# Re-timing three transfers of a recurrent attention step: query transposes, normed rows, value copies

## The chip, the cores and the metric

The kernel runs on one core of one Trainium2 chip. The metric is the device time of one execution in microseconds (us), as the median of several runs. Beside it stands one profiled execution, whose trace has every instruction of the engines (PE multiplies matrices, DVE and ACT do elementwise work, POOL and SP issue most of the transfers) and every packet of the 16 DMA engines.

## The reference

The input is one sequence of 2048 tokens of width 640. The first half of the layer is attention with a recurrent memory. The tokens are cut into 64 segments of 32. Each segment is joined with 8 memory rows, and attention with 32 heads of width 128 runs over these 40 rows. The output rows of the 8 memory places are the memory of the next segment, so the segments run one after another. The second half is a feed-forward block with a gate.

```python
for s in range(n_seg):
    h = jnp.concatenate([mem, xs], axis=1)      # 8 memory rows, 32 tokens
    q, k, v = (jnp.einsum('btd,dhe->bhte', h, W) for W in (Wq, Wk, Wv))
    scores = jnp.einsum('bhqe,bhke->bhqk', q, k) * scale
    o = jnp.einsum('bhqk,bhke->bhqe', _softmax(masked scores), v)
    o = jnp.einsum('bhte,hed->btd', o, Wo)
    mem = o[:, :M, :]
...
h = x + attention(layernorm(x)); h2 = h + W_down(relu(gate) * up)
```

(The weights' loop is drawn together here; the mask lets a row see the memory and the tokens up to itself.)

## The kernel before

The work is one program, written out for each engine as a list of operations. `_Graph.solve` (line 61) gives each operation the semaphore waits that it needs from the keys that it reads and writes: a write of a buffer waits until every earlier reader is done, and where the reader is a DMA, until the DMA has landed. Each engine runs its own operations in the order of the program text. There is no planner: the order in the text sets the order on each engine and in each DMA queue.

**The steps.** The loop at line 905 runs once per segment (a step). A step projects a tile of 32 columns, which holds the 8 memory rows and 24 "rider" tokens of later segments, because the memory is the only thing that the step has to wait for. So the keys, queries and values of ordinary tokens are made ahead of their segment and kept in rings of three segments: `Kr` (keys), `Qr` (queries), `Vr` (values). A block of 128 tokens is spread over four steps: 4 times 24 riders are 96, and the other 32 (the "extra" tokens, `act_e`) are projected in `extra_units` (line 858): their keys in the third step (s%4==2), their queries in the fourth, their values in the first step of the next block. In what follows, first to fourth step means s%4 = 0 to 3.

**One step in order.** PE projects the keys into two PSUM banks; ACT and DVE copy them to `tok[0]` and `tok[1]` (`to_tok`, line 429). SP transposes these 256 KB by DMA into `KS` (line 936), then the attention rows of the step before into `oT` (`trans_ox`, line 709). PE projects the queries, which go to `tok[2]` and `tok[3]`, and then the values, which go to `Vp`. `scores` (line 562) needs `KS`, and the ring slots of keys and queries of this segment. `exp_mem` (line 581) takes the exponentials of the memory's scores and masks them on DVE into `Pbd`: these are the memory probabilities. `exp_x` does the tokens' scores. Then `pv_mem`, the transposes of its result, `wo_pass` (line 638, 128 small matmuls) which gives the next memory, and `pv_x` (line 680) for the tokens.

**The rider queries.** `trans_q` (line 458) transposes `tok[2:4]` by DMA on SP's queue into `QS`, and `evac_q` (line 485) copies the riders from `QS` to `Qr` on ACT. In the first and second step (`qlate`) the transpose is issued at the end of the step and its evacuation is put on the list `late_k`, run in the next step behind the query copy. In the third and fourth step it is issued right behind `trans_ox` (line 949) and evacuated at the end of the value part (line 971).

**The rider values.** `v_riders` (line 492) issues DMAs from `Vp` to `Vr`: four, or eight where the 24 riders straddle two segments, as they do in the second and third step. All are issued by POOL.

**The extra keys.** In the third step, `evac` (line 874) copies the extra tokens' keys to `tok[2]` and `tok[3]`, and SP transposes them straight into `Kr`.

**The normed rows.** In the third step a block of input rows is normed on DVE (`row_scale`, line 382) into `xt`, and SP transposes it into `at` (line 1020), behind `pv_x` in the text; POOL copies it to the activations in the next step (`ln1_back`, line 518). For four blocks, in steps 32, 36, 40 and 44, the first step has a row block of the feed-forward part at the same place (`EARLY`, line 889).

**Instructions of PE.** `align` (line 138) pads PE's list with weight loads that do nothing, so that every 256th instruction falls at a chosen place of a step's `wo_pass` (`MARKS`, line 228).

Of the kernel before, what the change touches and what calls it, by code (L numbers as in the profile page):

```python
# [208 lines left out]
def build_kernel(nc, A_x, A_mem0, A_Wq, A_Wk, A_Wv, A_Wo, A_seg_len, B_W_gate, B_W_up, B_W_down, out):  # L209
    _, S, D = A_x.shape  # L210
    M = A_mem0.shape[1]
# [4 lines left out]
    NSEG = S // SEG  # L216
# [145 lines left out]
    def dma_t(dst, src, r, w):  # L362
        add("sp", lambda e: e.dma_start_transpose(dst, src), r=r, w=w, dma=True)
# [18 lines left out]
    def row_scale(src, skey, n, dst, dkey):  # L382
        add("dve", lambda v: v.tensor_scalar(dst[0:n, :], src[0:n, :], mv[0:n, 0:1], rs[0:n, 0:1], ALU.subtract,
                                             ALU.mult), r=[skey, ("mv",), ("rs",)], w=[dkey])
# [44 lines left out]
    def to_tok(b, t, eng):  # L429
        copy_op(eng, tok[t][:, :], bank(b), [B(b)], [("tok", t)])  # L430
# [58 lines left out]
    def seg_slot(s):  # L489
        return (s - 2) % (RING // SEG)  # L490

    def v_riders(t0, n, after=()):

        done = 0
        while done < n:
            t = t0 + done
            q, o = seg_slot(t // SEG), t % SEG
            m = min(n - done, SEG - o)
            for g in range(4):
                a, z = 32 * g + M + done, 32 * (g ^ 1) + o  # L500
                dma(Vr[q][z:z + m, :, :], Vp[a:a + m, :, :], r=[("Vp", 0), ("Vp", 1), ("Vp", 3), ("Vp1",), ("Vr1", q)] + list(after),
                    w=[("Vr", q, g, o)], eng="pool")
            done += m

    def vr_keys(q):
# [75 lines left out]
    def exp_mem():  # L581
        add("act", lambda a: a.activation(ap(om, 0, [[8, 2], [16, 8], [1, 8]]), s_view(0, M), ACTF.Exp,
                                          scale=SCALE), r=[B(P0), B(P1)], w=[("om",)])
        for i in range(2):
            add("dve", lambda v, i=i: v.tensor_tensor(ap(Pbd, 256 * i, [[32, 8], [16, 2], [1, 16]]),
                                                      ap(om, 0, [[16, 8], [0, 2], [1, 16]]),
                                                      ap(mbd, 32 * i, [[0, 8], [16, 2], [1, 16]]), ALU.min),
                r=[("om",), ("mbd",)], w=[("Pbd", i)])

    def exp_x():  # L590
        add("act", lambda a: a.activation(ap(Px, 0, [[32, 2], [64, 8], [1, 32]]), s_view(M, M + SEG),  # L591
# [83 lines left out]
    def store_attn(src, skey, s):  # L675

        dma(bass.AP(attn_d, SEG * s * D, [[160, 4], [D, SEG], [1, 160]]), src[:].rearrange("p c j -> p (c j)"), r=[skey],
            w=[("attn", s)], eng="pool")
# [179 lines left out]
    def extra_units(s):  # L858

        b, r = (s - 2) // 4, (s - 2) % 4
        t0 = 64 + 128 * b + 96
        if b < 0 or r == 3 or t0 >= S:
            return None, None, None
        a, ks = act_e[b % 2], [("acte", b % 2)]
        q = seg_slot(t0 // SEG)
        j = (1, 0, 2)[r]

        def part(n):
            project(a, ks, j, (0, 1), BQ, PARTS[n], j // 2)

        def evac():
            for i, e in enumerate(("act", "act")):
                if j == 2:
                    to_v(BQ[i], Vr[q], i, ("Vr", q), e)
                else:
                    to_tok(BQ[i], 2 + i, e)
            if j == 1:  # L880
                dma_t(Kr[q][:].rearrange("p h t -> p (h t)").rearrange("p (k r) -> p k r", r=128), tokp[1][:, :],
                      [("tok", 2), ("tok", 3)], [("Kr", q)])

        def fin():
            trans_q()
            late_q.append(lambda: evac_q(QS, ("QS",), t0, 32, 0, "act"))
        return part, evac, (fin if j == 0 else None)
# [17 lines left out]
    for s in range(NSEG):  # L905
# [20 lines left out]
        if s > 0:  # L926
            a, ks, kn = pass_act(s)
            t0, nr = rider_tokens(s)
            project(a, ks, 1, (0, 1), BQ, (0, 1), spare=16)
            ks = ks + kn  # L930
            project(a, ks, 1, (0, 1), BQ, (2, 3, 4), spare=24)
            to_tok(BQ[0], 0, "act")
            to_tok(BQ[1], 1, "dve")
            if last:
                break
            dma_t(KS[:].rearrange("p h t -> p (h t)").rearrange("p (k r) -> p k r", r=128), tokp[0][:, :],
                  [("tok", 0), ("tok", 1)], [("KS",)])
            trans_ox()
            for f in late:
                f()  # L940
            late = []
            project(a, ks, 0, (0, 1), (P0, P1), spare=40)
            to_tok(P0, 2, "act")
            to_tok(P1, 3, "dve")
            for f in late_k + late_q:
                f()
            late_k, late_q = [], []
            qlate = nr and s % 4 < 2
            if nr and not qlate and s < NSEG - 2:
                trans_q()  # L950
            loads()
            project(a, ks, 2, (0, 1), (P2, P3), (0, 1), spare=16)
            if s == NSEG - 2:
                trans8(tok[2], ("tok", 2), tok[3], ("tok", 3), T0)
                copy_op("dve", Qr[:, :, q, 0:M], slots(T0, 0, M), [B(T0)], [("Qm", q)])
                evac_q(slots(T0, 0, SEG), B(T0), t0, nr, M, "act")
            else:
                pick_mem(T0)
                copy_op("dve", Qr[:, :, q, 0:M], bank(T0)[:, 0:256].rearrange("p (h t) -> p h t", t=M), [B(T0)], [("Qm", q)])
            if nr:  # L960
                evac_k(KS, ("KS",), t0, nr, M, "dve")
            project(a, ks, 2, (0, 1), (P2, P3), (2, 3, 4), spare=24)
            to_v(P3, Vp, 1, ("Vp", 3), "dve")
            to_v(P2, Vp, 0, ("Vp", 0), "act", 0, 2)
            scores(s)
            exp_mem()
            to_v(P2, Vp, 0, ("Vp", 1), "act", 2, 4)
            exp_x()
            if nr:
                v_riders(t0, nr)  # L970
                if s < NSEG - 2 and not qlate:
                    evac_q(QS, ("QS",), t0, nr, M, "act")
        units, evac, nfin = extra_units(s)
        woe = s % 4 == 1 and s >= 5
# [1 line left out]
        def filler(n):  # L976
            if units:
                units(n)
            if woe:
                woe_pass(BQ[0], WPARTS[n])  # L980
# [12 lines left out]
        n = n_rows(nb) if s % 4 == 2 and ln else 128 if e2b is not None else 0  # L993
        if n:
            row_scale(xt, ("xt",), n, xt, ("xt",))
        filler(4)
        if evac:
            evac()
# [13 lines left out]
        if s >= 1:  # L1012
            wo_rows(T1, wtok[s % 2], ("wtok", s % 2), "act")
            store_attn(wtok[s % 2], ("wtok", s % 2), s - 1)
            if qlate and s < NSEG - 2:
                trans_q([("act", (s + 1) // 4 % 2, (s + 1) % 4, "m")])
                late_k.append(lambda t0=t0, nr=nr: evac_q(QS, ("QS",), t0, nr, M, "act"))
        pv_x(s, P0)
        if n:
            dma_t(chunks_of(at[:, :])[:, :, 0:n], xt[0:n, :], [("xt",)], [("at",)])  # L1020
            if s % 4 == 2:
                late.append(lambda nb=nb: ln1_back(nb, chunks_of(at[:, :]), [("at",)], "pool"))
        if nfin:
# [229 lines left out]
```

## Time and profile before

| | us |
|---|---|
| median of 3 runs | 1100.82 |
| lowest and highest run | 1099.63 and 1101.9 |
| profiled execution | 1100.57 |
| its span, first to last instruction | 1098.8 |
| PE busy | 1057.8 (96% of the span) |
| DVE, ACT, POOL busy | 608.4, 362.6, 291.5 |
| DMA moved | 121.60 MB |

The recurrence fills the span from about 50 to 911 us (the last `pv_x`, line 690, starts at 910.9); the feed-forward part follows. Lines are of kernel.py, and a helper's line stands for all of its uses: L464 and L466 are the copies on ACT and DVE, L360 is a plain DMA, L363 a transposing one, L400 and L422 are matmuls of the projections. "SPq" is SP's issue of a DMA: its length is that of the issue, not of the transfer. The table of DMA issues gives the median time from issue to landing.

### The profile page before, as it was taken

The page shows a single profiled execution, that of the slowest core. Times are in us where ns is not written, and L with a number is a line of the kernel's source. Part 1 is how long each engine was busy: PE and PEld are TensorE (multiplying, and loading weights), DVE is VectorE, ACT ScalarE, POOL GpSimd, SP SyncE. Part 2 cuts the span into 40 slices and gives each one's busy share as a digit, 9 for nine tenths or more (in the row PEclk, how much of TensorE's full clock was granted, in tenths as well). Part 3 has the DMA queues.
Part 4 walks back from the last instruction along what each step waited for, and adds up shares of the span by engine and source line. Part 5 has one row for each costly group of instructions (what it writes and reads, how often), then busy time and mean ns, then how long its engine had stood idle before and what let it go on. Part 6 is the DMA issues. An engine that isn't in the chain of part 4 may idle for free.

```text
span 1098.8 us, 55766 instructions
## 1 busy us (share of the span) xinstructions
PE 1057.8 (96%) x27875; PEld 511.8 (47%) x23292; DVE 608.4 (55%) x1673; ACT 362.6 (33%) x792; POOL 291.5 (27%) x585
## 2 busy tenths in 40 slices
PE   4789999999999999999999999999999999999999
PEld 2454545444545444545444544444445455444444
DVE  3245656565656565666656665565656554553522
ACT  1213333333433433333333333333333332231211
POOL 1023233333333232323232323242323243000000
PEclk9989999999999999999999999999999999999999
DMA  9946464546464545556556556554455548132100
GB/s 360 387 91 113 87 108 88 104 90 104 91 101 90 103 90 100 94 109 111 112 104 112 108 112 107 101 97 93 94 101 93 92 96 313 43 80 72 31 18 24
DMA packets 285882, 121.60 MB, mean 111 GB/s; under 512 B 261392, under 2 KB 275300, under 8 KB 285648
## 3 DMA queue, kind: packets, MB, share of 16 engines
q1 hardware_dynamic: 265920, 93.92, 40.9%
q0 software_dynamic: 19312, 23.86, 9.6%
q8 instruction: 201, 3.29, 1.3%
q14 instruction: 33, 0.27, 0.1%
q10 hardware_dynamic: 416, 0.26, 0.1%
HBM read 36.79 MB, written 7.19 MB: 40 GB/s over the span
## 4 chain that ended last, share of the span: by engine, by line
PE 90%; DMA 5%; SPq 3%; DVE 1%; issue 1%; ACT 0%; DVEq 0%
PE ps L422 25%; PE ps L400 23%; PE ps L644 13%; PE ps L1051 11%; PE ps L666 3%; PE ps L690 3%; PE ps L572 3%; SPq L360 3%; PE ps L1092 3%; DMA Wo<-in_A_Wo_dram 3%; PE ps L609 2%; PE ps L453 2%; DMA QS<-tok 1%; DMA KS<-tok 1%; PE ps L624 1%
## 5 line engine op out<-in xcount | busy, mean ns | idle before, releaser
L422 PE MATMUL ps<-W,act_r 128*32 128x512 bf16 x4292 | 404.8, 385 | 6.5 <-DMA W<-in_A_Wv_dram 2.6
L400 PE MATMUL ps<-W,act_r 128*32 128x512 bf16 x3588 | 359.0, 379 | 0.0
L360 POOL DMA_DIRECT2D Vr<-Vp x376 | 187.2, 505 | 345.5 <-ACT Px L591 280.6
L422 PEld LDWEIGHTS ps<-W,act_r 128*32 128x32 bf16 x4292 | 126.0, 97 | 257.7 <-issue 157.2
L464 ACT ACTIVATE tok<-ps 128x512 bf16<-128x512 f32 x192 | 110.8, 593 | 228.4 <-PE ps L400 200.4
L644 PE MATMUL ps<-Wo,oT 128*32 128x160 bf16 x8064 | 156.9, 235 | 6.2 <-DMA Wo<-in_A_Wo_dram 3.1
L466 DVE CAST tok<-ps 128x512 bf16<-128x512 f32 x131 | 90.5, 691 | 130.1 <-PE ps L400 109.5
L644 PEld LDWEIGHTS ps<-Wo,oT 128*32 128x32 bf16 x8064 | 143.8, 98 | 26.6 <-DVE oT L466 16.8
L422 PE MATMUL ps<-W,act_e 128*32 128x512 bf16 x900 | 89.8, 381 | 0.0
L400 PE MATMUL ps<-W,act_e 128*32 128x512 bf16 x900 | 89.4, 379 | 0.0
L555 DVE STREAM_TRANSPOSE TBf<-ps 128x64 f32<-128x64 f32 (+1 forms) x128 | 33.6, 263 | 93.2 <-PE ps L644 93.2
L705 DVE TENSOR_TENSOR ox<-ps,rx 128x512 bf16<-128x512 f32 x128 | 82.5, 686 | 2.2
L464 ACT ACTIVATE Qr<-QS 128x512 bf16<-128x512 bf16 (+3 forms) x107 | 69.7, 680 | 38.4 <-DMA QS<-tok 38.4
L360 POOL DMA_DIRECT2D attn_d<-wtok x62 | 46.4, 748 | 130.8 <-ACT wtok L464 130.8
L464 ACT ACTIVATE Vp<-ps 128x256 bf16<-128x256 f32 (+1 forms) x126 | 48.5, 385 | 81.5 <-PE ps L400 79.0
L1066 DVE TENSOR_TENSOR hT<-g,ps 128x512 bf16<-128x512 bf16 (+1 forms) x56 | 38.5, 688 | 47.3 <-PE ps L1051 43.4
L1051 PE MATMUL ps<-xn2T,Wg 128*128 128x512 bf16 x260 | 64.6, 379 | 0.0
L1051 PE MATMUL ps<-xn2T,Wu 128*128 128x512 bf16 x260 | 64.6, 379 | 0.0
L1064 ACT ACTIVATE g<-ps 128x512 bf16<-128x512 f32 (+1 forms) x56 | 32.4, 592 | 91.6 <-PE ps L1051 91.6
L466 DVE CAST Vp<-ps 128x512 bf16<-128x512 f32 x64 | 44.2, 691 | 28.3 <-PE ps L400 22.3
L1092 PE MATMUL ps<-Wd,hT 128*128 128x320 bf16 x210 | 57.2, 299 | 0.0
L400 PE MATMUL ps<-Wd,hT 128*128 128x320 bf16 x210 | 57.2, 299 | 0.0
(121 smaller groups left out, 1151.8 us busy)
## 6 DMA issues: line engine op xcount, KB each, us to landing
Vr<-Vp POOLq DMA_DIRECT2D x124, 48.8 KB, 1.9
W<-in_A_Wk_dram SPq DMA_DIRECT2D x2, 2560.0 KB, 13.4
W<-in_A_Wq_dram SPq DMA_DIRECT2D x2, 2560.0 KB, 29.0
W<-in_A_Wv_dram SPq DMA_DIRECT2D x2, 2560.0 KB, 27.7
Wo<-in_A_Wo_dram SPq DMA_DIRECT2D x2, 2560.0 KB, 28.5
xt<-in_A_x_dram SPq DMA_DIRECT2D x30, 160.0 KB, 2.7
Vr<-Vp POOLq DMA_DIRECT2D x128, 32.5 KB, 2.3
at<-attn_d SPq DMA_DIRECT2D x16, 160.0 KB, 3.4
```

The costliest lines, as they stand in the source:

```text
L360: add(eng, lambda e: e.dma_start(dst, src), r=r, w=w, dma=True)
L400: return pe.add_instruction(mybir.InstMatmult(name=nc.get_next_instruction_name(), engine=mybir.EngineType.PE, ins=[pe.lower_ap(rhs), pe.l ...
L422: ins = pe.matmul(*a, start=(c == 0), stop=(c == DC - 1), skip_group_check=True)
L464: add("act", lambda a: a.activation(dst, src, ACTF.Copy), r=r, w=w)
L466: add("dve", lambda v: v.tensor_copy(dst, src), r=r, w=w)
L555: add("dve", lambda v, lo=lo, hi=hi: v.transpose(TBf[:, lo:hi, :].rearrange("p c t -> p (c t)"), src[:, 32 * lo:32 * hi]), r=[wkey], w=[(" ...
L572: i = pe.matmul(bank((P0, P1)[g % 2])[p:p + (M if a else 32), 40 * k:40 * k + 40], lh, Qr[:, h, q, :], start=True, stop=True, skip_group_c ...
L644: i = pe.matmul(bank(bk)[32 * gg:32 * gg + 32, 0:160], src[:, hb, :], w[:, gg], start=(hb == ORDER[0]), stop=(hb == ORDER[31]), skip_group ...
L705: add("dve", lambda v, kh=kh: v.tensor_tensor(ox[:, :, kh, :], src[:, :, kh, 0:128], ap(rx, kh, [[2, 4], [0, 128]]), ALU.mult), r=[B(b0 + ...
L1051: ins = pe.matmul(bank(bk), w[:, c, lo:lo + 128], xn2T[par][:, :, c, :], start=(c == 0), stop=(c == DC - 1))
L1066: add("dve", lambda v: v.tensor_tensor(hT[par][lo:128, j, :], g1[gi][lo:128, :], bank(bu)[lo:128, :], ALU.mult), r=[B(bu), ("g1", gi)], w= ...
L1092: i = pe.matmul(*a, start=(j == 0), stop=(j == FC - 1), skip_group_check=True)
```

## The change

Four edits, all of order and place:

- The third step's query transpose (`qmid`) is issued behind `v_riders` and waits in addition for the second mask of the memory probabilities (the new key `qgo`). Its evacuation moves to `late_k`, in the next step.
- The extra keys go through `tok[0]` and `tok[1]`; the extra queries stay in `tok[2]` and `tok[3]`.
- The transpose of the normed rows is issued right behind their `row_scale`, which is ahead of the extra keys' transpose in SP's queue, and in steps 32 to 44 ahead of the late query transpose.
- In the second step every other rider value copy is issued by SP, so four of the eight.

```diff
-    def v_riders(t0, n, after=()):
+    def v_riders(t0, n, after=(), engs=("pool",)):
...
-                    w=[("Vr", q, g, o)], eng="pool")
+                    w=[("Vr", q, g, o)], eng=engs[g % len(engs)])
...
-                r=[("om",), ("mbd",)], w=[("Pbd", i)])
+                r=[("om",), ("mbd",)], w=[("Pbd", i), ("qgo", i)])
...
-                    to_tok(BQ[i], 2 + i, e)
+                    to_tok(BQ[i], 2 * (1 - j) + i, e)
             if j == 1:
-                dma_t(Kr[q][:].rearrange("p h t -> p (h t)").rearrange("p (k r) -> p k r", r=128), tokp[1][:, :],
-                      [("tok", 2), ("tok", 3)], [("Kr", q)])
+                dma_t(Kr[q][:].rearrange("p h t -> p (h t)").rearrange("p (k r) -> p k r", r=128), tokp[0][:, :],
+                      [("tok", 0), ("tok", 1)], [("Kr", q)])
...
             qlate = nr and s % 4 < 2
-            if nr and not qlate and s < NSEG - 2:
+            qmid = nr and s % 4 == 2 and s < NSEG - 2
+            if nr and not qlate and not qmid and s < NSEG - 2:
                 trans_q()
...
             if nr:
-                v_riders(t0, nr)
-                if s < NSEG - 2 and not qlate:
+                v_riders(t0, nr, (), ("pool", "sp") if s % 4 == 1 else ("pool",))
+                if qmid:
+                    trans_q([("qgo", 1)])
+                if s < NSEG - 2 and not qlate and not qmid:
                     evac_q(QS, ("QS",), t0, nr, M, "act")
...
             row_scale(xt, ("xt",), n, xt, ("xt",))
+            dma_t(chunks_of(at[:, :])[:, :, 0:n], xt[0:n, :], [("xt",)], [("at",)])
         filler(4)
         if evac:
             evac()
...
+            if qmid:
+                late_k.append(lambda t0=t0, nr=nr: evac_q(QS, ("QS",), t0, nr, M, "act"))
...
         pv_x(s, P0)
         if n:
-            dma_t(chunks_of(at[:, :])[:, :, 0:n], xt[0:n, :], [("xt",)], [("at",)])
```

## The prediction

> **What bounds the kernel now.** I read the page first (busy time, DMA issues), then the waits of PE, then SP's timeline over two steps with the DVE, ACT and POOL rows beside it, and last the busy time of four whole steps. From the page:
>
> ```profile
> PE 1057.8 (96%) x27875; PEld 511.8 (47%) x23292; DVE 608.4 (55%) x1673; ACT 362.6 (33%) x792; POOL 291.5 (27%) x585
> ...
> q8 instruction: 201, 3.29, 1.3%
> ...
> QS<-tok SPq DMA_TRANSPOSE x76, 3.1
> KS<-tok SPq DMA_TRANSPOSE x62, 3.2
> ...
> at<-xt SPq DMA_TRANSPOSE x19, 4.9
> Kr<-tok SPq DMA_TRANSPOSE x15, 5.2
> ```
>
> PE is the bound. No edit touches a matmul, so only stalls of PE can move. The extra keys' transpose (Kr) and the normed rows' (at) take 5.2 and 4.9 us to land, where QS and KS take 3.1 and 3.2. The busy time of steps 29 to 32, each window from the first pv_x matmul (line 690) of the step before to its own:
>
> ```profile
> 438.48:451.81 13.33, 13.33 (x438) 7.24 (x380) 8.15 (x24) 4.09 (x9) 4.62 (x9) 1.00 0.42 76
> 451.81:466.06 14.25, 13.78 (x422) 6.67 (x337) 8.98 (x26) 6.15 (x15) 5.99 (x12) 1.00 0.52 102
> 466.06:479.32 13.26, 13.26 (x421) 6.07 (x338) 7.56 (x21) 4.85 (x10) 3.40 (x9) 1.00 0.73 128
> 479.32:492.60 13.28, 13.28 (x418) 6.14 (x338) 9.32 (x26) 5.45 (x12) 3.58 (x7) 1.00 0.57 105
> ```
>
> The columns are window, length, then busy time of PE, PEld, DVE, ACT, POOL. The second line is a third step (s%4==2): it has PE idle of 0.47 us. Measuring every step between its line 690 starts in the same way, the shortest of each kind is 13.23, 13.29, 13.23 and 13.25 us (s%4 = 0 to 3); over steps 2 to 61, what lies above those floors sums to 1.9, 4.4, 6.4 and 4.7 us. So 17.4 us is all that any re-timing in the recurrence can win. PE's waits name it:
>
> ```profile
> PE ps L644 <- issue: 2.3, 7, 0.6
> PE ps L453 <- DVE tok L466: 1.9, 3, 1.0
> PE ps L572 <- DMA KS<-tok: 1.5, 3, 0.7
> ...
> PE ps L422 <- issue: 1.2, 4, 0.3
> ```
>
> The "issue" waits always stand at the same few places of a step, the middle of wo_pass and early in the K projection. SP's queue through a third step and into the fourth:
>
> ```profile
> 459.14 1.23 SPq L363 DMA_TRANSPOSE QS<-tok  x1
> 464.71 1.23 SPq L363 DMA_TRANSPOSE Kr<-tok  x1
> 466.04 1.91 SPq L363 DMA_TRANSPOSE at<-xt  x1
> 469.80 1.39 SPq L363 DMA_TRANSPOSE KS<-tok  x1
> ```
>
> and what these meet on DVE, ACT and POOL (the rows are from three engines' timelines):
>
> ```profile
> 464.28 0.44 DVE L383 TENSOR_SCALAR xt<-xt,mv,rs 128x640 bf16<-128x640 bf16 x1
> 469.07 0.69 DVE L466 CAST tok<-ps 128x512 bf16<-128x512 f32 x1 [0.61 <-PE ps L400]
> 463.55 1.08 ACT L464 ACTIVATE tok<-ps 128x512 bf16<-128x512 f32 x2 [0.33 <-PE ps L400]
> 462.04 3.99 POOL L360 DMA_DIRECT2D Vr<-Vp  x8 [0.80 <-ACT Px L591]
> ```
>
> The extra keys are in tok at 464.63, the normed rows in xt at 464.72: 0.09 us apart. The next step's key copies (DVE and ACT) write tok at 469.07, and KS is issued from them at 469.80.
>
> [...]The 201 instruction packets carry 3.29 MB, 16.4 KB each, [...]so I read the "issue" stalls as refills[...]. [...]The trace has 3.99 us of POOL for eight Vr copies. [...]Kr, issued under the tail of those eight copies, lands in 5.2 us.
>
> **The change, part by part.** The profiled run took 1100.57 us: the span of 1098.8 and 1.8 outside it. The median of the runs shown is 1100.82, 0.25 more. I sum against the profiled run.
>
> *Half of the second step's value copies to SP.* Eight issues of 0.5 us on POOL (3.99) become four there and four on SP, where a plain DMA issue takes 0.41 to 0.57. SP is idle from the oT issue to the QS issue in the next step's first us, so nothing queues behind. The copies have left about 2 us sooner, and less traffic stands before the refill that ends early in the third step. Its K projection loses 3.1 us in all to that stall (0.66, 0.39, 0.66, 0.40, 0.69 and smaller ones). Bounds: 0 (the refill is late for QS itself) to -3.1. I take -1.5.
>
> *Third step's QS to the memory probabilities.* It leaves SP at about 461.75 (the second mask of Pbd ends at 461.69) and not at 459.14. Its evacuation moves to the next step, behind the query copy at 471.23 + 0.60, two copies of 0.93 together, so done at 472.8 before the scores at 473.59: covered by 0.8 us. ACT no longer waits for QS in this step. In five of the 15 third steps QS landed about 2 us late and Kr went out at 13.8 to 14.6 us into the step, not 12.3; the next steps then lost 0.2 to 0.5. It also stands in wo_pass stalls of 0.36 three times and a tok wait of 1.05. Bounds: 0 to -3. I take -2. But QS now starts just before the eight Vr copies and shares the engines with them. The mask gains a write key, so the next step's mask carries one more wait, long fulfilled: nothing.
>
> *Normed rows ahead, in early-store steps too.* In steps 32, 36, 40 and 44 the transpose of xt leaves at 12.2 us of the step and no longer behind QS at 1.9 us of the next. It used to land around 7 us there and hold up KS; the steps after lost 0.81, 2.10, 0.33 and 0.83. Bounds: 0 to -4.1. I take -2.5 (KS then lands in 3.2, the 2.10 is mostly a late refill).
>
> *Extra keys through tok 0 and 1, behind the normed rows.* This is the new wait. Kr now reads the half of tok that the next step's keys are written to first. Before it read the other half, written at 471.23, 2.2 us later. Follow step 30: the rows go out at 464.72 + 0.06 = 464.78; SP needs 1.26 for one issue (the row of Kr to the row of at, less the gap), so Kr leaves at 466.04, where the rows did. Landing: 469.14 at the 3.1 us of a lone transpose, 470.3 at 4.3, 471.2 at Kr's own 5.2. The key copies want tok at 469.07. From then: copy 0.69, issue 0.04, KS 3.1 to 3.2, so KS lands 3.9 us after Kr and the scores want it at 473.59; it landed at 472.91 before (469.80 + 3.11). Slack 0.68. Stall of PE: 0, 0.6 and 1.5 us. In a step without a stall of its own the rows are ready 0.95 us ahead of the step's end (here 1.34), which adds 0.4. Where SP's issue of the first transpose takes 2.3 to 2.6 (about half of the third steps), Kr leaves another 1.1 late. Behind KS on SP is oT, and behind the key copies on ACT and DVE are the query copies, all shifted with PE. Bounds per step: 0 to 2.7; I take 1.2, at a landing of 4.3, a mean issue delay of 0.2 and the 0.4. There are 15 such steps (Kr x15): +18. Stalls that the fourth steps had ahead of their scores, about 2 us, are swallowed: -2.
>
> Sum: -1.5 - 2 - 2.5 + 18 - 2 = +10, so 1100.57 + 10 = 1110.6; I say 1110.
>
> **Rivals.** *Kr lands in time.* If QS and the rows take the whole collision with the Vr copies, Kr runs alone in 3.1 us and the stall is 0 to 0.2. For it: Kr lands in 3.07 when it leaves after the last Vr copy. Against: POOL's store of attn rows follows at 467.45, and the second transpose in this place took 3.2 to 5.0. Then the three gains stand with little against them: -6 + 1 = about 1096. This ends on the other side; it decides below 0.6 us a step, where 9 us of loss meet 8 of gain. *It cancels:* stalls of about 0.5 us, 1099 to 1102. *A backlog:* QS pushes the Vr copies into rows and Kr, Kr lands 6 us and more late, 2 us a step: -8 + 30, 1122. That the change does nothing can't be: the tok half that is waited for is another.
>
> **How the numbers follow.** Forecast (stall of 0.7 to 1.6 a step, 1103 to 1117) 0.50; backlog 0.16; cancels 0.10; Kr in time 0.24. About 0.2%, 2.2 us, is what a measurement tells from no change. Slower 0.66, same 0.10, faster 0.24. The range, 1095 to 1123, leaves out the ends of the two outer cases; for the slower cases alone it is 1103 to 1123.
>
> **What would show it.** Right: the fourth step's key copies idle on Kr's landing, KS goes out 1 to 2 us later than 3.74 us into the step, PE's wait at line 572 for KS grows from 1.5 to some 15 us in 15 or more places; the third steps' own excess falls from 6.4, and KS waits after the early-store steps vanish. Wrong: Kr's landing under 4 us, or no wait on tok ahead of the key copies.

## The result and the profile after

The changed kernel takes 1137.96 us (median of 4 runs, 1129.03 to 1139.9), the kernel before 1101.18 us (4 runs, 1099.63 to 1101.9). The ratio is 1.0320, with a 95% interval of 1.0265 to 1.0376: the change costs some 35 us. The direction was forecast, the size was not: 1110 was predicted, and the end of the range was 1123. The profiled execution took 1137.86 us, with a span of 1136.1 us.

The page of the kernel after, busy time and the chain that ended last:

```profile
PE 1061.9 (93%) x27875; PEld 519.3 (46%) x23292; DVE 607.0 (53%) x1673; ACT 359.4 (32%) x792; POOL 260.3 (23%) x521
...
PE 79%; DMA 15%; SPq 3%; DVE 2%; issue 2%; ACT 0%; DVEq 0%
```

PE's busy time is nearly the old one (1061.9, 1057.8 before), its share of the span fell from 96% to 93%. What was added is waiting, and the chain says for whom: DMA holds 15% of it, where it held 5% before, with `Kr<-tok` (6%) and `KS<-tok` (4%) as its largest entries.

PE's waits in the kernel after (us in total, times, longest):

```profile
PE ps L453 <- DVE tok L466: 23.5, 16, 2.6
PE ps L572 <- DMA KS<-tok: 11.6, 15, 1.0
...
PE ps L422 <- issue: 3.0, 8, 0.6
...
PE ps L644 <- issue: 2.5, 7, 0.6
```

The first two were 1.9 and 1.5 us. They are one stall taken in two pieces: first PE wants the query copies (line 453 transposes the memory's queries), which stand behind the late key copies on DVE and ACT, then it wants KS (line 572 is `scores`). The "issue" stalls sum to 5.5 us; before, these two rows had 3.5.

The medians from issue to landing in the kernel after:

```profile
at<-xt SPq DMA_TRANSPOSE x19, 5.6
Kr<-tok SPq DMA_TRANSPOSE x15, 5.4
```

The trace has the landing of six of the 15 Kr transfers; their median is hardly longer than before (5.2), that of the rows is (4.9). Steps 30 and 31 (third and fourth) of the kernel after, with the columns of the table in the prediction:

```profile
470.11:483.20 13.09, 13.09 (x420) 5.97 (x336) 8.99 (x26) 5.22 (x13) 5.59 (x11) 1.00 0.56 103
483.20:500.63 17.43, 14.25 (x422) 6.11 (x336) 7.47 (x21) 5.46 (x12) 4.62 (x11) 0.90 0.60 108
```

The third step is shorter than before's (14.25, the second line of that table). The fourth is 17.43 us long where it was 13.26 (the third line); PE has 422 records (421 before), 3.2 us of idle time where it had none, and a granted clock of 0.90, at which its busy time grew from 13.26 to 14.25. SP's queue through these two steps:

```profile
479.25 1.46 SPq L363 DMA_TRANSPOSE QS<-tok  x1
482.27 2.44 SPq L363 DMA_TRANSPOSE at<-xt  x1
484.75 1.32 SPq L363 DMA_TRANSPOSE Kr<-tok  x1
491.12 1.23 SPq L363 DMA_TRANSPOSE KS<-tok  x1
```

and what waits (timelines of DVE, ACT and PE in the same kernel):

```profile
490.40 1.29 DVE L466 CAST tok<-ps 128x512 bf16<-128x512 f32 x2 [4.79 <-DMA Kr<-tok]
490.39 1.09 ACT L464 ACTIVATE tok<-ps 128x512 bf16<-128x512 f32 x2 [6.08 <-DMA Kr<-tok]
491.75 0.37 PE L453 MATMUL ps<-ident,tok 128*128 128x32 bf16 x8 [2.54 <-DVE tok L466]
```

Step 31 starts at 483.20. Kr leaves 1.55 us into it and has landed when DVE and ACT go on at 7.2. Both engines wait for nothing but that landing; KS leaves at 7.9 and not at 3.74.

Where the time is, in sums over whole steps (each from its first line 690 start to the next; us, before and after):

| steps | before | after | difference |
|---|---|---|---|
| first, 4 to 60 | 200.4 | 200.1 | -0.3 |
| second, 5 to 61 | 203.8 | 205.2 | +1.3 |
| third, 2 to 58 | 204.8 | 202.2 | -2.7 |
| fourth, 3 to 59 | 203.5 | 244.1 | +40.6 |
| 1, 62, 63 and the start | 98.1 | 96.4 | -1.7 |

The sum is the difference of the spans (37.3, but for rounding). The whole loss stands in the 15 fourth steps: 2.7 us in each, of which 2.2 us are idle time of PE (34.6 us in the 15 steps, 1.6 before) and 0.5 us are longer busy time (209.5 us, 201.9 before).

### The profile page after: what moved, and what is told of

It reads as the page before. It is cut to its first block, busy times and chain, and to the rows that moved or that the text cites. A ratio compares the mean times of both kernels' runs of the same rounds, so it can differ in the third digit from the quotient of the medians.

```text
span 1136.1 us, 55782 instructions
## 1 busy us (share of the span) xinstructions
PE 1061.9 (93%) x27875; PEld 519.3 (46%) x23292; DVE 607.0 (53%) x1673; ACT 359.4 (32%) x792; POOL 260.3 (23%) x521
## 4 chain that ended last, share of the span: by engine, by line
PE 79%; DMA 15%; SPq 3%; DVE 2%; issue 2%; ACT 0%; DVEq 0%
PE ps L422 20%; PE ps L400 19%; PE ps L644 13%; PE ps L1056 10%; DMA Kr<-tok 6%; DMA KS<-tok 4%; PE ps L666 3%; PE ps L572 3%; SPq L360 3%; PE ps L1097 3%; DMA Wo<-in_A_Wo_dram 2%; PE ps L690 2%; PE ps L609 2%; DMA QS<-tok 1%; PE ps L453 1%
## 5 line engine op out<-in xcount | busy, mean ns | idle before, releaser
L422 PE MATMUL ps<-W,act_r 128*32 128x512 bf16 x4292 | 411.2, 383 | 9.8 <-issue 3.0
L400 PE MATMUL ps<-W,act_r 128*32 128x512 bf16 x3588 | 366.5, 381 | 0.0
L422 PEld LDWEIGHTS ps<-W,act_r 128*32 128x32 bf16 x4292 | 134.5, 97 | 254.4 <-issue 130.2
L360 POOL DMA_DIRECT2D Vr<-Vp x312 | 156.7, 509 | 397.4 <-ACT Px L591 328.6
L1069 ACT ACTIVATE g<-ps 128x512 bf16<-128x512 f32 (+1 forms) x56 | 32.5, 593 | 91.6 <-PE ps L1056 91.6
L572 PEld LDWEIGHTS ps<-Qr,Kr 128*32 128x32 bf16 x2048 | 39.0, 94 | 40.2 <-issue 39.9
L1097 PE MATMUL ps<-Wd,hT 128*128 128x320 bf16 x210 | 57.2, 299 | 0.0
## 6 DMA issues: line engine op xcount, KB each, us to landing
Vr<-Vp POOLq DMA_DIRECT2D x96, 32.5 KB, 4.5
```

Source lines behind the costliest of these rows:

```text
L360: add(eng, lambda e: e.dma_start(dst, src), r=r, w=w, dma=True)
L400: return pe.add_instruction(mybir.InstMatmult(name=nc.get_next_instruction_name(), engine=mybir.EngineType.PE, ins=[pe.lower_ap(rhs), pe.l ...
L422: ins = pe.matmul(*a, start=(c == 0), stop=(c == DC - 1), skip_group_check=True)
L572: i = pe.matmul(bank((P0, P1)[g % 2])[p:p + (M if a else 32), 40 * k:40 * k + 40], lh, Qr[:, h, q, :], start=True, stop=True, skip_group_c ...
L1097: i = pe.matmul(*a, start=(j == 0), stop=(j == FC - 1), skip_group_check=True)
```

## The experiments

Each ratio is to runs of the kernel before on the same chip; its median there was between 1096.03 and 1101.18 us, so times of different groups are compared by their ratios. The next table gives the mean over the 15 fourth steps of each profiled execution, in us from the step's start (a minus: in the step before). "Kr leaves" is the start of SP's issue; "key copies" and "scores" are the first start of each in the step. Kr's landing is the mean of those that the trace has: 12 of the 15 in before and only_tok, 14 in only_rows, 3 in other_source, 5 or 6 in the others. Where the key copies wait for Kr, their start, which is there for all 15, follows the landing by less than 0.1 us.

| kernel | ratio (95%) | Kr leaves | Kr landed | key copies | scores | length |
|---|---|---|---|---|---|---|
| before | 1 | -0.52 | 4.08 | 3.14 | 7.74 | 13.57 |
| after | 1.0320 (1.0265-1.0376) | 0.89 | 6.32 | 6.40 | 10.43 | 16.27 |
| other_source | 1.0008 (0.9989-1.0028) | 1.00 | 6.27 | 3.40 | 8.11 | 13.85 |
| only_tok | 1.0064 (1.0047-1.0082) | -0.99 | 3.98 | 4.13 | 8.26 | 14.04 |
| keys_first | 1.0124 (1.0083-1.0166) | -1.06 | 4.73 | 5.00 | 9.03 | 14.78 |
| keys_store_late | 1.0128 (1.0100-1.0156) | -1.02 | 4.48 | 4.63 | 8.66 | 14.48 |
| store_late | 1.0198 (1.0154-1.0242) | 0.81 | 5.25 | 5.23 | 9.25 | 15.08 |
| undo_query | 1.0316 (1.0257-1.0374) | 0.39 | 4.95 | 5.16 | 9.21 | 14.82 |
| only_rows | 1.0141 (1.0101-1.0180) | 0.53 | 5.45 | 3.05 | 8.44 | 14.08 |
| three_gains | 1.0313 (1.0281-1.0345) | 2.30 | 7.35 | 5.00 | 10.11 | 15.83 |
| gains_no_wait | 0.9997 (0.9979-1.0014) | -1.02 | 4.76 | 3.41 | 7.93 | 13.69 |

**other_source: the same transfers without the wait.** Kr's transpose reads a constant part of the weights; what this kernel leaves out is that the extra keys reach the ring, and no copy to tok has to wait for that transfer.

```diff
-                if j == 2:
+                if j == 1:
+                    copy_op(e, tok[i][:, :], bank(BQ[i]), [B(BQ[i])], [("tok", i), ("xk", i)])
+                elif j == 2:
...
-                dma_t(Kr[q]..., tokp[0][:, :], [("tok", 0), ("tok", 1)], [("Kr", q)])
+                dma_t(Kr[q]..., W[:, 1, 0, 0:1024], [("xk", 0), ("xk", 1)], [("Kr", q)])
```

> The changed kernel, with the extra keys' transpose reading a constant part of W in place of tok (so its ring keys are wrong numbers): all transfers are as large and leave in the same order, but nobody waits for this one before writing tok. Theory that the wait on tok carries the whole loss: no wait of ACT or DVE on Kr, KS goes out 3.7 us into the fourth step, 1098 to 1104 us. Rival (the crowd of transfers costs PE itself, through late refills and a late KS): over 1110.

Measured: 1098.18 us, ratio 1.0008 (0.9989 to 1.0028). The whole loss is gone. SP's queue in this kernel around the start of step 31 (465.11):

```profile
464.18 2.19 SPq L363 DMA_TRANSPOSE at<-xt  x1
466.41 1.31 SPq L363 DMA_TRANSPOSE Kr<-W  x1
468.85 1.23 SPq L363 DMA_TRANSPOSE KS<-tok  x1
```

Kr leaves 1.30 into the step, about as late as after, and lands as late (6.27, the mean of three), but KS leaves at 3.74, as before. So the late transfers as such cost nothing in sum (the fourth steps are still 0.28 us longer than before, the third steps 0.45 us shorter); the wait of the key copies on Kr's landing carries the loss.

**only_tok: that wait alone.** The kernel before, with the extra keys through tok 0 and 1; Kr still leaves ahead of the rows.

```diff
-                    to_tok(BQ[i], 2 + i, e)
+                    to_tok(BQ[i], 2 * (1 - j) + i, e)
-                dma_t(Kr[q]..., tokp[1][:, :], [("tok", 2), ("tok", 3)], [("Kr", q)])
+                dma_t(Kr[q]..., tokp[0][:, :], [("tok", 0), ("tok", 1)], [("Kr", q)])
```

> The kernel before with the extra keys through tok 0 and 1 and nothing else; they still go ahead of the rows. Kr landed 4.1 us into the fourth step before (mean), the key copies want tok at 3.0, and KS has 0.7 us to spare: a wait of about 1.1 us, of which 0.4 to 0.5 reach PE in each of 15 steps: +5 to +8 us, 1101 to 1106 beside a before of 1096. Rival, that the half of tok alone carries the loss: over 1120. Rival, that the slack hides it: no change.

Measured: 1106.78 us, ratio 1.0064 (1.0047 to 1.0082), which is 7 us. The fourth steps grow by 0.47 us, 7.0 in all. The wait costs a fifth of the loss when Kr leaves at -0.99; the rest is how late the other edits make Kr.

**keys_first: the order in SP's queue.** The kernel after, with the normed rows' transpose issued behind the extra keys' and not ahead of it.

```diff
             row_scale(xt, ("xt",), n, xt, ("xt",))
-            dma_t(chunks_of(at[:, :])[:, :, 0:n], xt[0:n, :], [("xt",)], [("at",)])
         filler(4)
         if evac:
             evac()
+        if n:
+            dma_t(chunks_of(at[:, :])[:, :, 0:n], xt[0:n, :], [("xt",)], [("at",)])
```

> The changed kernel with the rows' transpose behind the extra keys' in SP's queue again; the other edits stay. Kr then leaves about 1.0 us before the fourth step and not 0.9 us into it. If the order of these two is what turns the shared half of tok into a loss: Kr lands 4 to 5 us into the step, 1103 to 1115. If the query transpose under the value copies is the cause: Kr still lands at 6 and more, over 1125.

Measured: 1114.6 us, ratio 1.0124 (1.0083 to 1.0166). Undoing the order gives back 0.020, some 22 us: the largest single share. Kr leaves 1.95 us earlier (-1.06 for 0.89), the key copies start 1.4 earlier, and the fourth steps are 1.5 us shorter. The first expectation held.

**store_late: the attention store in Kr's way.** The kernel after, with POOL's store of attention rows at the end of the third step held until the fourth step's KS has landed.

```diff
...
-            store_attn(wtok[s % 2], ("wtok", s % 2), s - 1)
+            if s % 4 == 2 and s < NSEG - 2:
+                late.append(lambda s=s: store_attn(wtok[s % 2], ("wtok", s % 2), s - 1, [("KS",)]))
+            else:
+                store_attn(wtok[s % 2], ("wtok", s % 2), s - 1)
```

> The changed kernel with the third step's store of attention rows (wtok to attn_d, which POOL issues 1.4 us into the next step) held until KS of that step has landed. Theory of a collision: a transpose whose packets meet that store lands about 2.3 us late (5.5 to 5.7 in place of 3.1 to 3.4), and Kr, which leaves 0.2 to 1.7 us into the fourth step, meets it each time: without it Kr lands 4 to 5 us into the step in place of 6.3, 1110 to 1120 us. Rival (the eight value copies and the query transpose alone make Kr late): Kr still at 6 and more, 1133 to 1140.

Measured: 1123.39 us, ratio 1.0198 (1.0154 to 1.0242). Kr leaves as late as after (0.81) but lands 1.07 us earlier. POOL issues that store at 1.40 us of a step; in the kernel after, Kr leaves up to 1.2 us ahead of it in nine steps and 0.1 to 0.3 us behind it in six. The meeting costs some 13 us (0.012). Both ranges of the expectation were missed, between them: the store is a part of the lateness and not all of it.

**keys_store_late: both undone.** keys_first and store_late together.

> The kernel after with two things undone: the normed rows are behind the extra keys, and the attention store of the fourth step waits for its keys' transpose. If the oversize of the loss is the sum of the later issue of Kr (rows ahead) and of the meeting with the store, this stands at what the wait on tok costs alone, as in only_tok: 1.003 to 1.008, with Kr landing at about 4.0 us of the fourth step. If the query move adds its own delay, because its transpose pushes POOL's value copies into Kr, Kr lands at 4.5 us or later, and it is 1.009 to 1.014.

Measured: 1110.57 us, ratio 1.0128 (1.0100 to 1.0156). With Kr ahead of the rows, holding the store back changes nothing that the ratio can tell (1.0124 in keys_first, 1.0128 here), though Kr lands 0.25 us earlier; and the second expectation holds: Kr leaves at -1.02 as in only_tok but lands at 4.48 and not at 3.98. What differs from only_tok beside the store is the query move, the SP copies and the early rows; so 0.006, some 7 us, is for these three together. Half of it (0.003) is what the early rows cost alone (early_rows, below), the copies cost nothing alone (only_sp). That the rest is the query transpose, which pushes POOL's value copies into Kr, fits the landing and the copies' own time (4.1 us, 2.5 in only_tok); it is argued, not shown.

**undo_query: the query move alone taken back.** The kernel after with `qmid = False`.

```diff
-            qmid = nr and s % 4 == 2 and s < NSEG - 2
+            qmid = False
```

> The changed kernel with the third step's query transpose and its evacuation back at their old place; the other three edits stay. Theory of a backlog (the query transpose, issued just ahead of eight value copies, is slowed by them and slows all that follows it): the query transposes land in about 3.1 us again, Kr in 4 to 5 and no longer in 5.2 to 6.5, and the fourth steps lose about 1.2 us each to the wait on tok, not 2.7: 1108 to 1118 us. Rival (the order of rows and extra keys and the shared half of tok alone cost what was measured): 1133 to 1140.

Measured: 1127.13 us (1118.8 to 1135.83), ratio 1.0316 (1.0257 to 1.0374). By that ratio the move's return gives nothing back; by the medians (1127.13 to 1096.03, and 1137.96 to 1101.18) the ratio falls from 1.033 to 1.028, some 5 us. The profiled execution is the shortest of the four, with a span of 1117.1 us where the kernel after had 1136.1, and it shows what the first expectation said: Kr lands at 4.95, 4.6 us after it leaves, and the fourth steps are 1.25 us longer than before, not 2.7. POOL's value copies (issue to landing, here and in the kernel after) show the backlog itself:

```profile
Vr<-Vp POOLq DMA_DIRECT2D x96, 32.5 KB, 2.1
```

```profile
Vr<-Vp POOLq DMA_DIRECT2D x96, 32.5 KB, 4.5
```

Copies of this size took 3.8 to 4.7 us (medians) in seven kernels with the query move (after, other_source, store_late, keys_first, keys_store_late, three_gains, gains_no_wait) and 2.1 to 2.5 in six without it (before, undo_query, only_sp, only_rows, only_tok, early_rows). So the move does slow the value copies, and Kr lands later behind them in the execution that was traced (5.4 us after its issue in the kernel after, 4.6 here). How much of the 35 us it carries stays open: the four runs are spread too widely to tell nothing from a good part.

**only_rows: the rows ahead, alone.** The kernel before, with the rows' transpose behind `row_scale`; Kr stays in tok 2 and 3.

```diff
             row_scale(xt, ("xt",), n, xt, ("xt",))
+            dma_t(chunks_of(at[:, :])[:, :, 0:n], xt[0:n, :], [("xt",)], [("at",)])
...
         pv_x(s, P0)
         if n:
-            dma_t(chunks_of(at[:, :])[:, :, 0:n], xt[0:n, :], [("xt",)], [("at",)])
```

> The kernel before with the transpose of the normed rows right behind their row_scale and nothing else (the extra keys still go through tok 2 and 3). The prediction's term: -2.5 us (0 to -4.1) from the steps after 32, 36, 40 and 44. Rival from the changed kernel's trace: in those steps the rows' issue pushes the query transpose by 0.2 to 0.3 us into the store of attention rows, it lands 2.7 us late and the copies to tok wait for it: 0 to +1. Kr lands about 1.3 us later in the third steps and nobody waits for it: no cost. 1098 to 1102 in all.

Measured: 1110.22 us, ratio 1.0141 (1.0101 to 1.0180). I had expected nothing to be lost. PE's waits in this kernel:

```profile
PE ps L453 <- DVE tok L466: 19.0, 16, 2.0
```

The old half of tok is waited for too: its next writers, the query copies, want it at 5.2 us of the fourth step. In five of the 15 steps Kr landed at 3.7 to 3.9, in the nine others that show it at 6.0 to 7.0, in part after the same issue times (0.23 gave 3.86, 0.24 gave 6.10), and then the query copies, PE's line 453 and the scores are late. The exchange of the halves isn't needed for a loss; the rows ahead are enough. Some 0.003 of the 0.0141 is what the rows ahead in steps 32 to 44 cost alone (early_rows, below); in the traces the second steps grow by 5.6 us and the fourth by 7.6.

**only_sp: the value copies alone.** The kernel before, with half of the second step's value copies on SP.

```diff
...
-                v_riders(t0, nr)
+                v_riders(t0, nr, (), ("pool", "sp") if s % 4 == 1 else ("pool",))
```

> The kernel before with half of the second step's value copies on SP and nothing else. The prediction's term: -1.5 us (0 to -3.1), 1098 to 1101. Rival, that the late refill in the third step's K projection stems from the query transpose itself: no change, and the same excess in third steps.

Measured: 1095.32 us, ratio 0.9998 (0.9983 to 1.0012). Nothing: the third steps sum to 204.7 us as before (204.8), and PE's "issue" stalls at lines 644 and 422 sum to 4.1 us, 3.5 before.

**three_gains: the parts that I had priced as gains.** The query move, the SP copies and the early rows of steps 32 to 44, on the kernel before; no exchange of the halves, and in the third steps the rows behind Kr. (The rows' part of the diff; the other two parts are as in the change.)

```diff
+            if s % 4 != 2:
+                dma_t(chunks_of(at[:, :])[:, :, 0:n], xt[0:n, :], [("xt",)], [("at",)])
...
-            dma_t(chunks_of(at[:, :])[:, :, 0:n], xt[0:n, :], [("xt",)], [("at",)])
             if s % 4 == 2:
+                dma_t(chunks_of(at[:, :])[:, :, 0:n], xt[0:n, :], [("xt",)], [("at",)])
```

> The kernel before with the query move, the value copies on SyncE and the normed rows ahead in the early-store steps 32, 36, 40 and 44; in the third steps the normed rows stay behind pv_x, and the extra keys stay in tok 2 and 3. These are the three parts that my prediction priced as gains. If its prices hold, 1.5 + 2 + 2.5 = 6 us are won: a ratio of 0.994 to 0.996, the third steps' excess down by about 3 us and the query copies' wait gone after the early-store steps. Rival, from the runs so far: none of the three gains, because each only exchanges which transfer meets POOL's copies and store; then 0.998 to 1.006, and the query copies of the fourth steps wait on Kr, which leaves behind a later QS, in some steps.

Measured: 1133.33 us, ratio 1.0313 (1.0281 to 1.0345). Both expectations fell. The waits of all engines in this kernel, and then its timelines of ACT and PE at the start of step 31 (481.26):

```profile
ACT tok L464 <- DMA QS<-tok: 87.1, 19, 6.1
```

```profile
482.13 1.08 ACT L464 ACTIVATE tok<-ps 128x512 bf16<-128x512 f32 x2 [4.62 <-DMA QS<-tok]
483.36 0.40 PE L422 MATMUL ps<-W,act_r 128*32 128x512 bf16 x4 [1.45 <-ACT tok L464]
```

The late query transpose reads tok 2 and 3 until it lands, in step 30 at 13.9 us of the step, and here the extra keys are copied to the same half. They wait 4.6 us, PE waits for their copy in the next step's key projection, and Kr leaves only at 2.30. So the exchange of the halves isn't a separate edit: it takes the extra keys out of the moved query transpose's way, and puts them into the way of the next step's keys.

**gains_no_wait: the same parts, with neither half waited for.** keys_first and other_source together.

> The kernel after, with the normed rows behind the extra keys (as in keys_first) and the extra keys' transpose reading a constant part of the weights (as in other_source): the ring's extra keys are wrong numbers, every transfer has its size and place. What is left of the change is the query move, the value copies on SyncE and the early rows of steps 32 to 44, without a wait on either tok half. If the three gains of my prediction exist, their 6 us show here: 0.994 to 0.997. Rival: they are 0 and the transfers only exchange places: 0.999 to 1.003. If the query move itself costs time (its evacuation in the next step), over 1.003.

Measured: 1096.93 us, ratio 0.9997 (0.9979 to 1.0014). The third steps do get shorter, 199.5 us where they had 204.8; the second and fourth together give back 2.9. In the ratio there is no gain. So even without any wait on Kr the three parts together are worth nothing that can be measured. One of them costs 0.003 when it stands alone (early_rows, next), so another may have won about as much; no run has the query move free of both waits and without the early rows.

**early_rows: the early-store term alone.** The kernel before, with the rows ahead in steps 32, 36, 40 and 44 only (the diff of three_gains without its query move and SP copies).

> The kernel before with the normed rows' transpose ahead in steps 32, 36, 40 and 44 alone. My prediction gave this -2.5 us (0 to -4.1): 0.996 to 0.998. Rival: nothing is won, because the late query transpose behind the rows now meets the attention store that POOL issues at 1.4 us of the next step, lands at 5.5 us and not 3.1, and the query copies there wait for it: 0.999 to 1.001.

Measured: 1100.93 us, ratio 1.0031 (1.0016 to 1.0047): a loss of 3.4 us where I had -2.5. The timelines of SP, DVE and PE in this kernel, step 45 (from 656.20):

```profile
657.15 1.30 SPq L363 DMA_TRANSPOSE QS<-tok  x1
662.79 0.69 DVE L466 CAST tok<-ps 128x512 bf16<-128x512 f32 x1 [2.88 <-DMA QS<-tok]
663.54 0.36 PE L453 MATMUL ps<-ident,tok 128*128 128x32 bf16 x8 [1.34 <-DVE tok L466]
```

The late query transpose, now the second in the queue, stands close to the store that POOL issues 1.40 us into the step and lands after 5.55 us; the query copies wait for it. Whether the store or the rows ahead of it slow it is not separated: no run holds the store here. The four steps behind the early stores sum to 58.9 us, 57.2 before, which is half of the 3.4.

**before_store_late.** The kernel before, with the store held behind KS in all steps.

> The kernel before with every store of attention rows held until the next KS has landed. If the store's collision with transposes costs the kernel before something too (the rows and Kr in the first us of fourth steps, and the late refills there): 0 to -6 us, 1090 to 1096 beside a before of 1096. Rival: the store then meets other transfers, or stands ahead of POOL's next work: 0 to +5.

Measured: 1099.03 us, ratio 0.9999 (0.9968 to 1.0030). In the kernel before, as far as a ratio known to 0.003 tells, the store is in nobody's way that PE waits for.

**rows_late, rows_late_sp, after_rows_late: the rows behind KS.** If the rows' transpose troubles Kr, it can go later: behind the next step's `trans_ox`, at 6.7 us of the fourth step (on the kernel before, on that with the SP copies, and on the kernel after, where it is 7.6).

```diff
-            dma_t(chunks_of(at[:, :])[:, :, 0:n], xt[0:n, :], [("xt",)], [("at",)])
+            late.append(lambda n=n: dma_t(chunks_of(at[:, :])[:, :, 0:n], xt[0:n, :], [("xt",)], [("at",)]))
```

> The kernel before with the rows' transpose the other way: behind the next step's KS and oT, where its reader (a copy on POOL for a step two later) still has time. If the rows' transpose in the first us of the next step delays Kr, KS and the refills there: the fourth steps that had KS at 7.6 to 8.0 us have it at 7.0, the steps after 32, 36, 40 and 44 lose less than 0.3 us each, -2 to -5 us, ratio 0.995 to 0.998. Rival: it only moves the meeting to the query transpose behind it, 0.999 to 1.003.

> The same with half of the second step's value copies on SP as well. Alone that edit gave nothing (ratio 0.9998), so the same as rows_late within 0.2%. If the two share a bottleneck, up to 2 us better.

> The changed kernel with the rows' transpose behind the next step's KS and oT. The extra keys then have SP and the transposes to themselves after the query transpose: Kr leaves 1.0 us before the fourth step and, if the rows are what holds it up, lands 3 to 4 us into it: 1100 to 1108, ratio 1.002 to 1.008. If the query transpose and the eight value copies still hold it up (as where the extra keys went first: Kr landed 5.8 us after its issue), ratio 1.010 to 1.016.

Measured: 1105.78 us, 1.0070 (1.0047 to 1.0092); 1109.29 us, 1.0086 (1.0053 to 1.0118); 1127.78 us, 1.0285 (1.0237 to 1.0333). The first two are slower than before, not faster, and the third lies above both of its ranges; only the forecast that the SP copies add nothing to rows_late held (0.16%). The fourth steps do gain (200.7 us for 203.5 in rows_late, 14.04 a step for 16.27 on the kernel after), and the first steps lose: 208.6 us for 200.4 in rows_late, 219.0 in after_rows_late. The loss moves one step on.

No kernel here beats the kernel before.

## Why the prediction was right in direction and wrong in size

**Half of the second step's value copies to SP, -1.5.** It was 0 (only_sp, -0.2 us, -1.9 to +1.3). The "issue" stalls that it was to shorten stayed in only_sp (4.1 us, 3.5 before), and in the kernel after they sum to 5.5. The term reads them as late refills and counts on less traffic ahead of one. That they are refills fits the trace of the kernel before: each of the 12 such stalls of PE between 60 and 912 us ends 1.3 to 1.8 us after the end of a 16.4 KB instruction packet. That traffic makes one late was my estimate and is not shown: the DMA engines' busy share in the 1.5 us ahead of those 12 packets was 0.52, ahead of the other 176 in that time 0.54.

**Third step's QS, -2.** The mechanism was there: the third steps fell by 2.7 us after, and by 5.3 in gains_no_wait, which has the query move and the SP copies (the latter worth nothing). Whether any of it remains in the kernel's time is open (gains_no_wait has nothing in sum, but with the early rows' loss in it). The step left out what the later landing holds: in three_gains tok 2 and 3 until 13.9 us. The exchange of the halves avoids that, and the sum should have priced the two as one edit. It also named the sharing with the eight value copies and put no price on it; those copies took 4.5 us in place of 2.1 (undo_query).

**Normed rows ahead in the early-store steps, -2.5.** The wrong sign: +3.4 us alone. The step took the rows behind QS to be what held up KS, and said that KS would then land in 3.2 us. The edit puts QS behind the rows and closer to the attention store, and QS took 5.5 (3.1 before), so that the query copies waited for it.

**Extra keys through tok 0 and 1, +18.** The mechanism, its place and its formula were right: the key copies idle on Kr's landing, KS goes out 3.3 us later, PE waits at `scores` in 15 places (11.6 us), and takes the other part of the stall already at line 453, for the query copies that the prediction named as shifted. KS lands 4.1 us after Kr (10.45 and 6.32), where 3.9 was said. The step that failed is the sentence "I take 1.2, at a landing of 4.3, a mean issue delay of 0.2 and the 0.4": both sizes in it were too small, and the fourth steps grew by 2.7 us each. The larger error is the landing. Kr took 5.4 us, not 4.3, and that makes 1.1 of the missing 1.5 us. With the attention store held back it took 4.4 (store_late): the prediction names that store among the rivals and has no term for it in the sum. The smaller error is the issue delay. Two transposes stand in a row on SP, and in each of the 15 steps one of the two issues took 2 us or more and not 1.26: that of the rows in six steps, so that Kr left at 1.5 to 1.7, and Kr's own in the other nine. The prediction had seen the long first issue in "about half of the third steps", another 1.1 us each; that is 0.55 in the mean, and it took 0.2. With 0.55, its own departure comes to 0.9 us into the step (-0.02 for step 30, 0.4 and 0.55), and 0.89 was measured. With the measured numbers its formula gives 6.32 + 4.1 - 7.74 = 2.7. Times 15, that is 40 us.

**The sum.** The loss of the wait by itself is 7 us (only_tok). With the other edits, rows still behind Kr, it is 13.6 (keys_first, 0.0124). Rows ahead of Kr make it 35; of this step of 22, 13 go when the store is held back (store_late). These are not shares that add up: each was taken with the other edits in place, and all of them go when the wait goes (other_source). Of the 6 us of gains that stood against it, the first to third steps show 1.7 (the table in the section on the result).

**The rivals.** The backlog, at 1122 and 2 us a step, was the nearest: Kr does land "6 us and more late" in the step, though from an issue that is late as well. Its cause was QS. That QS slows the value copies is shown (4.5 us after, 2.1 in undo_query); how much it makes Kr late is open, and keys_first and store_late show that the order of the rows and the store matter beside it. "Kr in time" was wrong because it let QS and the rows take the whole collision: in none of the 15 steps did the key copies start before 5.38 us. "It cancels" needed stalls of 0.5.

**What would show it.** Seen: idle on Kr's landing ahead of the key copies, and the wait for KS in 15 places. Not seen: KS only 1 to 2 us late; stalls gone behind the early-store steps. The third steps' excess fell as said, from 6.4 to 3.7 us over the old floor.

What stays open: why Kr lands at 3.8 in some steps of only_rows and at 6 and more in others that leave at the same time; and how much of the loss is the query move's (the 3 to 4 us between only_tok and keys_store_late that the early rows don't account for, or more).

## What to carry to other kernels

When a transfer is moved, list who writes its source next, and price the landing from the new place in the queue: with the long issues ahead of it at their full share (in the kernel after one of two issues in a row took 2 us or more in all 15 steps, and not 1.26), and with the stores and copies that it will meet there (Kr took 5.4 us in the kernel after and 4.4 in store_late). In this program a buffer that a DMA reads is held until the landing (tok 2 and 3 until 13.9 us in step 30 of three_gains): moving one such read later and swapping halves to make room passed the wait to the next writer. In rows_late what was gained where the transfer was taken away (2.8 us in the fourth steps) was lost again elsewhere (8.2 us in the first), so a gain that is counted in one step must be looked for in the next ones too.

## What the runs showed of the hardware

**PE ran at half clock behind some of the stalls.** From step 2 on, the kernel before has no window of half clock; the kernel after has five of 3.41 us, four of them in fourth steps (19, 27, 31 and 47) and one in step 62. (Ahead of step 2 the kernel before has three, the kernel after one.) Two windows of the kernel after, around one of them (columns as above, the clock third from the end):

```profile
315.00:319.07 4.07, 1.68 (x37) 0.58 (x20) 1.72 (x3) 1.91 (x4) 1.12 (x4) 1.00 0.17 34
319.07:322.48 3.41, 2.90 (x92) 1.01 (x76) 1.59 (x5) 1.43 (x4) 0.02 (x1) 0.50 0.95 192
```

PE was idle for 2.4 us of the 4.07 ahead, and then ran at a granted clock of 0.50. In the 3.41 us ahead of the five windows PE was idle for 1.7 to 2.3 us. If the rest of the kernel after, from step 2 on, is laid out in stretches of 3.41 us end to end with these windows, two more stretches have as much idle time or nearly so (1.8 us in 605.79:609.20, 1.7 in 373.68:377.09), and the clock behind them was 1.00; so idle time alone does not tell which stall is followed by such a window. In the kernel before, laid out in the same way, no stretch from step 2 on has more than 1.3 us. At 0.50 a window of 3.41 us loses at most half of its length, so an estimate from the trace is up to 8.5 us for the five; the four fourth steps with such a window have 14.2 to 14.9 us of PE busy time, the other eleven 13.3 to 14.1. It also fits the spread of the kernel after: the run of 1129.03 us had a mean clock of 0.998, the others 0.988 to 0.991, and 0.007 of 1136 us is 8. The prediction had no term for it; in the fourth steps it is a part of the measured 2.7 us.

**The time to land was longer beside POOL's transfers.** In the kernel after, the 256 KB transpose of KS landed after 3.2 us (median). The third steps' query transpose, of the same size, landed after 5.9 to 8.0 us at its new place just ahead of the eight value copies (11 of 15, those that the trace has), and after 3.1 (median of 11, 3.1 to 5.4) at its old place in the kernel before. Kr took 5.4 us close to POOL's store (median of six, 4.0 to 6.6); store_late shows the store's part: 4.4 us with it held back. SP's issue of one transpose took 1.2 to 2.6 us in both kernels. Kr at -1 us landed after 5.0 us in only_tok and after 5.5 in keys_store_late. The copies suffered too: those of 32.5 KB took 4.5 us in the kernel after and 2.1 in undo_query, with the query transpose at its old place.
